# Keys' weights fused in 64x64 tiles at the head of a gated-mix kernel

## Chip, cores and metric

The kernel runs on one core of a Trainium2 chip. The metric is the device time of one execution in microseconds. The engines named below are TensorE (PE in the profile, its weight loads PEld), VectorE (DVE), ScalarE (ACT), GpSimd (POOL) and SyncE (SP), which here only issues DMAs. All are in order, each by its own instruction stream.

## What is computed

x has 2048 rows of 512. Two branches are mixed by a gate that each row computes from itself: a linear attention with 32 heads of 16, and a dense layer with Mish. Everything is fp32.

```python
x = A_x
g = sigmoid((x * gate_w).sum(-1, keepdims=True))
# a: attention
q, k, v = (x @ wqkv) split into 3 parts of 32 heads x 16
pq, pk = q @ w_phi[head], k @ w_phi[head]                  # 16x16 per head
phi_q = concat(softmax(pq), softmax(-pq)); phi_k = likewise of pk
kv = phi_k^T v; z = sum over rows of phi_k
a = ((phi_q kv) / (phi_q z + 1e-6)) @ wo
# b: dense
b = mish(x @ w1 + b1) @ w2
return g * a + (1 - g) * b
```

Only the head of the kernel changes. There the weights of the keys are multiplied by w_phi once ("fuse"), so that x @ (wk w_phi) gives pk directly; the same is done for the queries.

## The kernel before

**Splitting.** A product in fp32 is slower on TensorE than one in the fp32r form. So every operand X is split into a high part Xh (a copy rounded to fp32r, made on ACT) and a low part Xl = X - Xh (a subtraction, on DVE or POOL), and each product is made of three: Xh Wh, Xh Wl and Xl Wh, summed in one PSUM bank.

**Stages.** Stage A goes over 8 chunks of 256 rows of x. Each chunk makes k, v and q (12 products each for two tiles of 128 rows), the softmax features of k, and adds to kv. Stage B goes over 4 blocks of 512 rows: the features of q, the attention's output, and the dense branch. The instruction order within the stages is written out by hand as words (FIRST, EVEN, ... BLOCK); every word runs a step that was registered by `at`. `pin` keeps each instruction in the order of the program on its engine.

**The head**, which is all that the change touches:

- L141 to L165 issue the first loads. `bds` (the block-diagonal w_phi, 256 KB) goes out on ACT's queue. On SP's queue go, in this order, the keys' weights wkT in four parts of 256 KB (one for each 128 of the 512 inputs), with x's first chunk (`rawx[0]`, 512 KB, all four input parts) behind the first two; then wv in two pieces of 512 KB, the queries' weights wqT in four parts, and x's second chunk.
- L168 to L172: `ones` is filled on DVE, and `WARM` = 6 fp32 products of `ones` by `ones` run on TensorE into a PSUM bank that nobody reads. They need nothing but `ones`.
- `fuse(staged, k)` (L213) multiplies part k of the staged weights by bds: four fp32 products of 128x128, one for each group G of 8 heads, into the four quarters of one PSUM bank. `fsplit` (L681) then writes that bank to `wkh[:, k]` (ACT) and the rest to `wkl[:, k]` (DVE).
- `fuse_tiles(staged, ks)` (L219) does two parts of the queries' weights with 64x64 tiles instead: bds is block-diagonal with 16x16 blocks, so only the products of rows r..r+64 with columns r..r+64 of bds are not zero. Each group takes four products of 64x64 (two halves of the contraction, two halves of the output), which lie in four different quarters of the array. The two halves r go to two PSUM banks, and two parts k share the pair.
- `x_hi` and `x_lo` split one half j of x's chunk (two input parts, 128x512) on ACT and on DVE.
- `k_part(k)` (L688) adds input part k to the keys of both row tiles of the first chunk: for each tile Xh Wh, Xh Wl, Xl Wh, six products of 128x512 in all. The two sums stay in PSUM (`pk`) through all four parts.
- The order at L696 to L714: fuse 0, fsplit 0, both halves of x, fuse 1, fsplit 1, fuse 2, fsplit 2, k_part(0), fuse 3, fsplit 3, k_part(1), the splits of wv, k_part(2), k_part(3). `run(FIRST, ...)` follows, with `fq` (the queries' fuse) and v first.

**PSUM.** Eight banks of 128x512 in three pools: tag "a" has 3, "dn" 4, "kv" 1. The warm products and the keys' and queries' fuse use "dn" in turn, `pk` uses "a". A bank is written again only when its readers are done.

Of the kernel before, what the change touches and what calls it, by code (L numbers as in the profile page):

```python
# [15 lines left out]
P = 128  # L16
# [5 lines left out]
NG = 4  # L22
SC = 256
# [7 lines left out]
NF = NFA + NFB  # L31
GROW = FA % P
ORDER = [NFA - 1] + list(range(NFA - 1)) + list(range(NFA, NF))
WARM = 6

# [52 lines left out]
def tile_gated_mix(ctx: ExitStack, tc: tile.TileContext, xT, wv, wkT, wqT, bd, w1a, w1b, b1, w2a, w2b, wo, out):  # L90
# [6 lines left out]
    pin = tc.keep_in_program_order  # L97
    V, G_, A_, Sy = nc.vector, nc.gpsimd, nc.scalar, nc.sync

    def mm(*a, **k):  # L100
        return pin(nc.tensor.matmul(*a, **k))  # L101

    def T(shape, dt, tag, bufs, name):
        nm[0] += 1
        return sp.tile(shape, dt, name=f"{name}_{nm[0]}", tag=tag, bufs=bufs)

    def k8(name, tag, dt=F32R):
        return T([P, 2048], dt, tag, 1, name)

    def k4(name, tag, dt=F32):  # L110
        return T([P, 1024], dt, tag, {"E": 4, "tx": 2, "oh": 2, "z": 1}[tag], name)

    def k2(name, tag, dt=F32):
        return T([P, 512], dt, tag, {"pq": 3, "io": 4, "hl": 8}[tag], name)

    def psum(name, tag, bufs={"a": 3, "dn": 4, "kv": 1}):
        nm[0] += 1
        return pp.tile([P, 512], F32, name=f"{name}_{nm[0]}", tag=tag, bufs=bufs[tag])

    def act(out_, in_, fn=AF.Copy, **k):  # L120
        return pin(A_.activation(out_, in_, fn, **k))  # L121

    def kt(t, f):
        return t[:, : KT * f].rearrange("p (k f) -> p k f", f=f)
# [4 lines left out]
    def f32(ap):  # L129
        return ap.bitcast(F32)  # L130
# [5 lines left out]
    def stage(wT):  # L136
        return T([P, NFA * 512], F32, "w1a", 2, "wT")[:, : KT * 512].rearrange("p (k g f) -> p k g f", k=KT, f=P)

    skT, sqT = stage(wkT), stage(wqT)
    bds = k2("bds", "io")[:, :].rearrange("p (g f) -> p g f", g=NG)  # L140
    pin(A_.dma_start(bds, bd))  # L141
    rawx = {}

    def ldx(c):
        rawx[c] = k4("xraw", "tx")
        pin(Sy.dma_start(kt(rawx[c], SC), xT[c]))

    def ldk(dst, src, k):
        pin(Sy.dma_start(dst[:, k, :, :], src[:, k, :, :]))

    ldk(skT, wkT, 0)
    ldk(skT, wkT, 1)
    ldx(0)
    ldk(skT, wkT, 2)
    ldk(skT, wkT, 3)

    def piece(dram, o, n=1024):
# [9 lines left out]

    ones = k2("ones", "io")[:, :P]  # L168
    pin(V.memset(ones, 1.0))
    ps = psum("warm", "dn")  # L170
    for _ in range(WARM):
        mm(ps[:, :P], ones, ones, start=True, stop=True)  # L172
    onr = const.tile([P, P], F32R, name="onr")
    A_.preload_act_table_set("exp_and_others")
    act(onr, ones)
# [20 lines left out]
    def at(key, name, fn):  # L196
        steps.setdefault((key, name), []).append(fn)

    def run(text, key, prev=None, nxt=None):
# [6 lines left out]
    wkh, wkl, wvh, wvl, wqh, wql = [  # L206
        kt(k8(n, t), 512) for n, t in (("wkh", "xbh"), ("wkl", "xbl"), ("wvh", "woh"), ("wvl", "wol"), ("wqh", "tt"), ("wql", "eT"))]
    xs, Es, vs, psA = {}, {}, {}, {}
# [1 line left out]
    zacc = k4("zacc", "z")  # L210
    pin(G_.memset(zacc, 0.0))

    def fuse(staged, k):  # L213
        acc = psum("fuse", "dn")
        for G in range(NG):
            mm(acc[:, G * P : (G + 1) * P], staged[:, k, G, :], bds[:, G, :], start=True, stop=True)
        return acc

    def fuse_tiles(staged, ks):  # L219

        acc = [psum("fuse", "dn") for _ in range(2)]
        for i, k in enumerate(ks):
            for G in range(NG):
                o = (i * NG + G) * 64
                for r in (0, 64):
                    for c in (0, 64):
                        mm(acc[r // 64][c : c + 64, o : o + 64], staged[r : r + 64, k, G, c : c + 64], bds[r : r + 64, G, r : r + 64], start=True, stop=True, skip_group_check=True)
        return acc

    def proj(x, t, wh, wl, tag):  # L230
        ps = psum("proj", tag)
        xh, xl = x
        sl = slice(t * P, (t + 1) * P)
        n = 0
        for a, w in ((xh, wh), (xh, wl), (xl, wh)):
            for k in range(KT):
                mm(ps, a[k // 2][:, k % 2, sl], w[:, k, :], start=(n == 0), stop=(n == 3 * KT - 1))
                n += 1
        return ps
# [4 lines left out]
    def x_hi(c, j):  # L244
        act(xs[c][0][j], kt(rawx[c], SC)[:, 2 * j : 2 * j + 2, :])

    def x_lo(c, j, eng):
        pin(eng.tensor_sub(xs[c][1][j], kt(rawx[c], SC)[:, 2 * j : 2 * j + 2, :], f32(xs[c][0][j])))
# [189 lines left out]
    def mid_ops():  # L438
# [18 lines left out]
        def z():  # L457
            B["zb"] = k4("zb", "z")
            for a in range(2):
                ps = psum("z", "dn")  # L460
                for j in range(2):
                    mm(ps, onr, B["zs"][j][:, a * 512 : (a + 1) * 512], start=(j == 0), stop=(j == 1))
                act(B["zb"][:, a * 512 : (a + 1) * 512], ps)
# [212 lines left out]
        b_ops(b)  # L676


    acc = {}

    def fsplit(h, l, k):  # L681
        act(h[:, k, :], acc[k])
        pin(V.tensor_sub(l[:, k, :], acc[k], f32(h[:, k, :])))

    new_x(0)
    pk = {}

    def k_part(k):  # L688
        for t in range(2):
            sl = slice(t * P, (t + 1) * P)  # L690
            if t not in pk:
                pk[t] = psum("proj", "a")
            for n, (a, w) in enumerate(((xs[0][0], wkh), (xs[0][0], wkl), (xs[0][1], wkh))):
                mm(pk[t], a[k // 2][:, k % 2, sl], w[:, k, :], start=(k == 0 and n == 0), stop=(k == KT - 1 and n == 2))

    acc[0] = fuse(skT, 0)  # L696
    fsplit(wkh, wkl, 0)
    for j in range(2):
        x_hi(0, j)
        x_lo(0, j, V)  # L700
    acc[1] = fuse(skT, 1)
    fsplit(wkh, wkl, 1)
    acc[2] = fuse(skT, 2)
    fsplit(wkh, wkl, 2)
    k_part(0)
    acc[3] = fuse(skT, 3)
    fsplit(wkh, wkl, 3)
    k_part(1)
    for j in range(2):
        h, l = [w[:, 2 * j : 2 * j + 2, :].rearrange("p k f -> p (k f)") for w in (wvh, wvl)]  # L710
        act(h, wvr[j])
        pin((V, G_)[j].tensor_sub(l, wvr[j], f32(h)))
    k_part(2)
    k_part(3)  # L714

    def fq():
        for j in range(2):
            acc["q", 2 * j], acc["q", 2 * j + 1] = fuse_tiles(sqT, (2 * j, 2 * j + 1))

    at(("A", 0), "fq", fq)  # L720
    for i in range(4):
        j, r = i // 2, i % 2
        wh, wl = [w[:, 2 * j : 2 * j + 2, :].rearrange("p k (g r f) -> p r (k g) f", r=2, f=64)[:, r, :, :] for w in (wqh, wql)]

        def ps(i=i):
            return acc["q", i][:, :].rearrange("p (g f) -> p g f", f=64)

        at(("A", 0), f"fh{i}", lambda wh=wh, ps=ps: act(wh, ps()))
        at(("A", 0), f"fl{i}", lambda wh=wh, wl=wl, ps=ps: pin(V.tensor_sub(wl, ps(), f32(wh))))
# [71 lines left out]
```

## Time and profile before

| | us |
|---|---|
| three runs | 451.97, 452.77, 452.78 |
| their median | 452.77 |
| the profiled execution | 452.07 |
| its span, first to last instruction | 450.3 |
| TensorE's first product (warm) | 1.12 |
| TensorE idle after the warm products | 4.05 to 5.82 |
| queries' fuse, first product | 16.44 |
| first product of v | 18.46 |
| end of TensorE's last product | 447.15 |

The profile's page begins with the busy time of each engine; the trace behind it can be asked for any stretch. A stretch's row gives the busy time and the number of instructions of each engine in it. The chain of waits follows the work that ended last backwards through whatever released each step. A group of instructions shows the tile that is written, the tiles that are read, their shapes, the count, the busy time with the mean duration of one in ns, and the idle time of the engine just before them with what ended it. In this trace an fp32 product appears as two matmul rows (two passes of the array), an fp32r product as one. Rows on TensorE overlap: a row of 0.39 us may be followed by the next one 0.227 us later, so I look at the distance from start to start.

### The profile page before, as it was taken

The page shows a single profiled execution, that of the slowest core. Times are in us where ns is not written, and L with a number is a line of the kernel's source. Part 1 is how long each engine was busy: PE and PEld are TensorE (multiplying, and loading weights), DVE is VectorE, ACT ScalarE, POOL GpSimd, SP SyncE. Part 2 cuts the span into 40 slices and gives each one's busy share as a digit, 9 for nine tenths or more (in the row PEclk, how much of TensorE's full clock was granted, in tenths as well). Part 3 has the DMA queues.
Part 4 walks back from the last instruction along what each step waited for, and adds up shares of the span by engine and source line. Part 5 has one row for each costly group of instructions (what it writes and reads, how often), then busy time and mean ns, then how long its engine had stood idle before and what let it go on. Part 6 is the DMA issues. An engine that isn't in the chain of part 4 may idle for free.

```text
span 450.3 us, 6996 instructions
## 1 busy us (share of the span) xinstructions
PE 444.3 (99%) x2778; PEld 363.6 (81%) x2778; DVE 305.7 (68%) x404; ACT 194.8 (43%) x265; POOL 162.8 (36%) x102
## 2 busy tenths in 40 slices
PE   7999999999999999999999999999999999999997
PEld 6888888888888888878787887887887888787885
DVE  2599459369399999997989976576967629611003
ACT  3544443344335555626265453534254553234221
POOL 3438777767952345521122212024212122221211
DMA  7721514605524100405244151331151302030002
GB/s 281 259 92 48 175 49 130 181 14 182 184 74 119 48 24 20 122 13 140 84 105 130 35 154 34 83 118 48 29 137 46 100 16 95 1 82 13 1 1 93
DMA packets 25737, 40.07 MB, mean 89 GB/s; under 512 B 5732, under 2 KB 14180, under 8 KB 25704
## 3 DMA queue, kind: packets, MB, share of 16 engines
q1 hardware_dynamic: 25384, 39.22, 28.8%
q8 instruction: 22, 0.36, 0.4%
q10 hardware_dynamic: 288, 0.39, 0.3%
q14 instruction: 11, 0.09, 0.1%
q0 software_dynamic: 32, 0.01, 0.0%
HBM read 22.82 MB, written 8.40 MB: 69 GB/s over the span
## 4 chain that ended last, share of the span: by engine, by line
PE 98%; DMA 1%; DVE 0%; issue 0%
PE proj L101 29%; PE up L101 27%; PE down L101 26%; PE wo L101 10%; PE num L101 2%; PE kvp L101 2%; PE fuse L101 2%; DMA bds<-in_bd_dram 1%; PE rest L101 0%; PE z L101 0%; DVE io L651 0%; PE kvT L454 0%
## 5 line engine op out<-in xcount | busy, mean ns | idle before, releaser
L498 POOL TENSOR_TENSOR l<-act,h 128x512 fp32r<-128x512 f32 x44 | 63.0, 1432 | 222.1 <-ACT h L121 183.6
L121 ACT ACTIVATE act<-up,b1s 128x512 f32<-128x512 f32 x44 | 30.3, 688 | 88.9 <-PE up L101 87.7
L318 POOL TENSOR_TENSOR zacc<-zacc,E 128x1024 f32<-128x1024 f32 x16 | 39.7, 2483 | 42.7 <-DVE E L280 32.6
L121 ACT ACTIVATE E<-E 128x1024 f32<-128x1024 f32 x32 | 33.6, 1059 | 47.7 <-DVE E L265 47.6
L280 DVE TENSOR_TENSOR E<-E,Sm 128x1024 f32<-128x1024 f32 x32 | 45.7, 1427 | 1.1
L269 DVE TENSOR_REDUCE Sm<-E 128x64 f32<-128x1024 f32 x32 | 38.7, 1210 | 5.0 <-ACT E L121 5.0
L101 PE MATMUL wo<-woh,ohl 128*128 128x512 f32 x128 | 40.7, 389 | 0.0
L101 PE MATMUL down<-w2ah,h 128*128 128x512 f32 x96 | 37.5, 390 | 0.0
L101 PE MATMUL down<-w2ah,l 128*128 128x512 f32 x96 | 37.4, 389 | 0.0
L101 PE MATMUL down<-w2al,h 128*128 128x512 f32 x96 | 37.3, 389 | 0.0
L256 DVE TENSOR_REDUCE mx<-proj 128x32 f32<-128x512 f32 x16 | 11.0, 689 | 30.7 <-PE proj L101 30.7
L101 PE MATMUL down<-w2bh,h 128*128 128x512 f32 x78 | 30.5, 390 | 0.0
L101 PE MATMUL down<-w2bl,h 128*128 128x512 f32 x78 | 30.4, 389 | 0.0
L101 PE MATMUL down<-w2bh,l 128*128 128x512 f32 x78 | 30.3, 389 | 0.0
L121 ACT ACT_TABLE_LOAD x19 | 24.4, 1283 | 10.1 <-PE up L101 9.8
L121 ACT ACTIVATE h<-act 128x512 fp32r<-128x512 f32 x44 | 27.8, 632 | 1.4
L610 DVE TENSOR_TENSOR ohl<-num,ohl 128x512 fp32r<-128x512 f32 x16 | 10.3, 682 | 26.5 <-ACT ohl L121 26.3
L101 PEld LDWEIGHTS wo<-woh,ohl 128*128 128x128 f32 x128 | 24.0, 188 | 5.0
L101 PE MATMUL up<-xbh,w1ah 128*128 128x512 f32 x96 | 26.2, 394 | 0.0
L101 PE MATMUL up<-xbh,w1al 128*128 128x512 f32 x96 | 25.7, 389 | 0.0
L101 PE MATMUL up<-xbl,w1ah 128*128 128x512 f32 x96 | 25.7, 389 | 0.0
L403 DVE TENSOR_TENSOR xbl<-xraw,xbh 128x1024 fp32r<-128x1024 f32 x8 | 12.2, 1563 | 19.8 <-ACT xbh L121 19.8
(121 smaller groups left out, 969.7 us busy)
## 6 DMA issues: line engine op xcount, KB each, us to landing
xraw<-in_xT_dram SPq DMA_DIRECT2D x16, 512.0 KB, 4.7
eT<-tt SPq DMA_DIRECT2D x128, 64.0 KB, 2.0
pqd<-qs SPq DMA_DIRECT2D x16, 256.0 KB, 3.0
pq<-pqd SPq DMA_DIRECT2D x16, 256.0 KB, 2.9
out_dram<-io SPq DMA_DIRECT2D x15, 256.0 KB, 2.1
raw<-in_w1a_dram SPq DMA_DIRECT2D x3, 512.0 KB, 4.5
raw<-in_w2a_dram SPq DMA_DIRECT2D x3, 512.0 KB, 3.8
wT<-in_wkT_dram SPq DMA_DIRECT2D x4, 256.0 KB, 5.5
```

Of the source, the lines that this page charges most:

```text
L101: return pin(nc.tensor.matmul(*a, **k))
L121: return pin(A_.activation(out_, in_, fn, **k))
L256: pin(V.tensor_reduce(d[name], hv(src()), axis=AX.X, op=op))
L269: pin(V.tensor_reduce(d["S"], hv(d["E"][:, :]), axis=AX.X, op=ALU.add))
L280: pin(eng.tensor_mul(hv(d["E"][:, :]), hv(d["E"][:, :]), d["S"][:, :, None].to_broadcast([P, 2 * H, DH])))
L318: at(key, f"z{t}", lambda d=d: pin(G_.tensor_add(zacc, zacc, d["E"])))
L403: pin(V.tensor_sub(xb[b][1][:, :, sl], kt(raw[h], SC), f32(xb[b][0][:, :, sl])))
L498: pin(G_.tensor_sub(U[i]["l"], U[i]["a"], f32(U[i]["h"])))
L610: pin(V.tensor_sub(ohl[h, gp][:, 512:], num[h, gp], f32(ohl[h, gp][:, :512])))
```

## The change

The keys' fuse is made of 64x64 tiles, as the queries' fuse is. `fuse` now does one part k of either into a pair of banks that the caller passes (`fuse_banks`), at the half of the columns that k's parity gives. The keys take a pair of their own for each part, though a part fills only the left or the right half of the two; the queries still put two parts into one pair. `fsplit` empties a part in two ACT copies and two DVE subtractions of 128x256, one for each bank, instead of one of each of 128x512.

x's first chunk is loaded in two halves, between the first three parts of wkT. Ten warm products run ahead of the fuse instead of six, and two more between the keys' parts 0 and 1. The bank of the warm products comes from pool "a".

The head's order is new: fuse 0, two warm products, fuse 1; half 0 of x, fsplit 0, half 1 of x, fsplit 1; k_part(0), k_part(1); fuse 2, fuse 3, fsplit 2, fsplit 3; the splits of wv, k_part(2), k_part(3). Within k_part the order is Xh Wh for both tiles, Xl Wh for both, Xh Wl for both. In the built program each engine's order behind the head is the old one. One DMA more is issued on SP, and since the DMAs share eight semaphores in turn, wv's second piece now waits on SP for the landing of bds, and each later load for the landing of another earlier one than before.

```diff
-WARM = 6
+WARM = 10
...
     ldk(skT, wkT, 0)
-    ldk(skT, wkT, 1)
-    ldx(0)
-    ldk(skT, wkT, 2)
+    rawx[0] = k4("xraw", "tx")
+    for j in range(2):
+        pin(Sy.dma_start(kt(rawx[0], SC)[:, 2 * j : 2 * j + 2, :], xT[0][:, 2 * j : 2 * j + 2, :]))
+        ldk(skT, wkT, j + 1)
     ldk(skT, wkT, 3)
...
-    ps = psum("warm", "dn")
-    for _ in range(WARM):
-        mm(ps[:, :P], ones, ones, start=True, stop=True)
+    pw = psum("warm", "a")
+
+    def warm(n):
+        for _ in range(n):
+            mm(pw[:, :P], ones, ones, start=True, stop=True)
+
+    warm(WARM)
...
-    def fuse(staged, k):
-        acc = psum("fuse", "dn")
+    def fuse(acc, staged, k):
+
         for G in range(NG):
-            mm(acc[:, G * P : (G + 1) * P], staged[:, k, G, :], bds[:, G, :], start=True, stop=True)
-        return acc
...
+            o = (k % 2 * NG + G) * 64
+            for r in (0, 64):
+                for c in (0, 64):
+                    mm(acc[r // 64][c : c + 64, o : o + 64], staged[r : r + 64, k, G, c : c + 64], bds[r : r + 64, G, r : r + 64], start=True, stop=True, skip_group_check=True)
+
+    def fuse_banks():
+        return [psum("fuse", "dn") for _ in range(2)]
+
+    def halves(w, ks):
+        return [w[:, ks, :].rearrange("p k (g r f) -> p r (k g) f", r=2, f=64)[:, r, :, :] for r in range(2)]
...
-    def fsplit(h, l, k):
-        act(h[:, k, :], acc[k])
-        pin(V.tensor_sub(l[:, k, :], acc[k], f32(h[:, k, :])))
+    def fsplit(acc, k):
+        wh, wl = halves(wkh, slice(k, k + 1)), halves(wkl, slice(k, k + 1))
+        src = [a[:, k % 2 * 256 : k % 2 * 256 + 256].rearrange("p (g f) -> p g f", f=64) for a in acc]
+        for r in range(2):
+            act(wh[r], src[r])
+        for r in range(2):
+            pin(V.tensor_sub(wl[r], src[r], f32(wh[r])))
...
     def k_part(k):
-        for t in range(2):
-            sl = slice(t * P, (t + 1) * P)
-            if t not in pk:
-                pk[t] = psum("proj", "a")
-            for n, (a, w) in enumerate(((xs[0][0], wkh), (xs[0][0], wkl), (xs[0][1], wkh))):
+        for n, (a, w) in enumerate(((xs[0][0], wkh), (xs[0][1], wkh), (xs[0][0], wkl))):
+            for t in range(2):
+                sl = slice(t * P, (t + 1) * P)
+                if t not in pk:
+                    pk[t] = psum("proj", "a")
                 mm(pk[t], a[k // 2][:, k % 2, sl], w[:, k, :], start=(k == 0 and n == 0), stop=(k == KT - 1 and n == 2))
 
-    acc[0] = fuse(skT, 0)
-    fsplit(wkh, wkl, 0)
-    for j in range(2):
-        x_hi(0, j)
-        x_lo(0, j, V)
-    acc[1] = fuse(skT, 1)
-    fsplit(wkh, wkl, 1)
-    acc[2] = fuse(skT, 2)
-    fsplit(wkh, wkl, 2)
-    k_part(0)
-    acc[3] = fuse(skT, 3)
-    fsplit(wkh, wkl, 3)
-    k_part(1)
+    for ks in ((0, 1), (2, 3)):
+        acc = []
+        for k in ks:
+            acc.append(fuse_banks())
+            fuse(acc[-1], skT, k)
+            if k == 0:
+                warm(2)
+        for k in ks:
+            if k < 2:
+                x_hi(0, k)
+                x_lo(0, k, V)
+            fsplit(acc[k % 2], k)
+        if ks[0] == 0:
+            k_part(0)
+            k_part(1)
...
     def fq():
         for j in range(2):
-            acc["q", 2 * j], acc["q", 2 * j + 1] = fuse_tiles(sqT, (2 * j, 2 * j + 1))
+            accq.extend(fuse_banks())
+            for k in (2 * j, 2 * j + 1):
+                fuse(accq[-2:], sqT, k)
```

## The prediction

> **What bounds the kernel now.** I read the page's first part, then stretches of the span chosen at the seams of the kernel's head, then the chain of waits over the first 20 us. Columns of the stretches: length, each engine's busy us and (instructions), granted clock, DMA share, GB/s.
>
> ```profile
> PE 444.3 (99%) x2778; PEld 363.6 (81%) x2778; DVE 305.7 (68%) x404; ACT 194.8 (43%) x265; POOL 162.8 (36%) x102
> ...
> 0.00:5.80 5.80, 2.93 (x12) 2.63 (x12) 0.17 (x1) 1.59 (x2) 3.58 (x13) 1.00 0.57 164
> 5.80:8.50 2.70, 2.68 (x12) 2.68 (x13) 0.00 (x0) 0.57 (x2) 0.00 (x0) 1.00 1.03 403
> 8.50:16.40 7.90, 7.90 (x46) 6.68 (x44) 5.01 (x7) 4.64 (x8) 1.38 (x1) 1.00 1.01 377
> 16.40:18.40 2.00, 2.00 (x129) 1.96 (x128) 0.14 (x1) 0.77 (x2) 1.09 (x1) 1.00 0.76 231
> 18.40:447.20 428.80, 428.75 (x2593) 349.62 (x2582) 299.90 (x396) 187.21 (x254) 156.71 (x88) 1.00 0.27 79
> 447.20:450.40 3.20, 0.00 (x0) 0.00 (x0) 0.47 (x1) 0.00 (x0) 0.00 (x0) 1.00 0.46 164
> ```
>
> TensorE is the bound without a gap: from 18.40 to 447.20 it is busy 428.75 of 428.80 us, and already from 5.82. The change touches only what comes before 18.4 us. So the question is how much sooner TensorE reaches the queries' fuse and, behind it, the first v product. Columns of the chain: start, us, what.
>
> ```profile
> 0.81 4.97 DMA bds<-in_bd_dram
> 5.78 0.04 issue
> 5.82 4.30 PE fuse L101 x24
> 10.13 1.40 PE proj L101 x6
> 11.52 0.89 PE fuse L101 x8
> 12.41 4.09 PE proj L101 x18
> 16.51 2.02 PE fuse L101 x128
> ```
>
> The fp32 fuse product is two passes of the array, so a part k of the keys' fuse is 4 products, 8 passes; a proj product is one pass. The last part took 0.89 us, 0.112 a pass. The first three took 4.30 for 24: in the single rows passes start 0.213 us apart until 8.54, then 0.112. The warm products, 12 passes in 2.93 us, also start 0.213 apart. So TensorE ran at 1/1.9 of its speed until 8.54, though the granted clock stands at 1.00 in every stretch; I go by the spacing. Proj products start 0.227 apart. The queries' fuse is already made of 64x64 tiles: 128 passes, four parts, in 2.02.
>
> Counted in slots (when TensorE can begin the next product), the keys' path runs from 5.82 to 16.35, the last proj's start at 16.12 plus 0.227.
>
> **The change, part by part.** The sum goes along TensorE's order, from 5.82.
>
> *Twelve warm products.* Ten stand ahead: 20 passes, first step 0.37, then 0.213, free at 5.55. That lies under the wait for bds, which lands at 5.78: cost nothing. Were they 0.3 us longer, that would be paid in full. A quicker clock only ends them sooner. Two more, 4 passes x 0.112 = 0.45, follow part 0.
>
> *64x64 tiles.* In the queries' fuse four passes start together every 0.0585, eight such steps a part: 0.47 instead of 0.89. Going in from proj costs 0.14 (slot 16.35; 32 steps later it ends at 18.36, 2.01 less 1.87), and coming out costs 0.24 (from 18.36 the eighth v product starts at 20.185 instead of 19.95). Both are paid three times more: around part 0, around part 1, around parts 2 and 3. Bounds of a pair: 0, if the next operand is waited for anyway, to 0.76, twice the row. I take 0.38.
>
> *x in halves.* SP now issues wkT 0, x half 0, wkT 1, x half 1, wkT 2, wkT 3.
>
> ```profile
> xraw<-in_xT_dram SPq DMA_DIRECT2D x3, 512.0 KB, 6.5
> wT<-in_wkT_dram SPq DMA_DIRECT2D x4, 256.0 KB, 5.5
> ...
> 0.80 0.87 SPq L149 DMA_DIRECT2D wT<-in_wkT_dram  x2
> 1.72 0.43 SPq L146 DMA_DIRECT2D xraw<-in_xT_dram  x1
> ```
>
> wkT 1 landed at 6.76, x at 1.72 + 6.5 = 8.21; the 512 KB of x took 1.45. Halved: x half 0 at 6.76, wkT 1 at 7.48, x half 1 at 8.21; wkT 2 and 3 as before. Behind it SP has one issue more (0.45): wv 0 goes out that much later, wv 1 now waits for bds's semaphore, 5.8 instead of 4.08, and the four wqT and x's second chunk follow it. That is free: by 5.80 only 5.80 x 164 GB/s = 0.95 MB of the 2.25 MB issued had moved, and the queues stay full for 3.2 us at 403 GB/s. Without that cover the last wqT (landed at 14.84, wanted at 16.9) has 2 us to lose.
>
> *Evictions in halves.* Each part leaves in two ACT copies and two DVE subtractions of 128x256 instead of one of each of 128x512: four more on each engine.
>
> ```profile
> L121 ACT ACTIVATE wkh<-fuse 128x512 fp32r<-128x512 f32 x4 | 2.4, 594 | 6.9 <-PE fuse L101 6.8
> L121 ACT ACTIVATE wvh<-raw 128x1024 fp32r<-128x1024 f32 x2 | 2.0, 1052 | 0.0
> L121 ACT ACTIVATE onr<-ones 128x128 fp32r<-128x128 f32 x1 | 0.3, 311 | 0.0
> ...
> L683 DVE TENSOR_TENSOR wkl<-fuse,wkh 128x512 fp32r<-128x512 f32 x4 | 2.7, 687 | 8.9 <-ACT wkh L121 8.9
> ```
>
> No 128x256 copy is in the trace. ACT: between 0.311 (128 columns) and 0.594 (512); on the line to 1.052, 0.38, and 0.29 from one start to the next (512 columns start 0.50 apart). DVE: between 0.165 (ones, 128 columns) and 0.687; on the line to wvl's 1.226, 0.42, and 0.33 apart instead of 0.60. The Trainium skill ("TensorEngine Tiling (Array Packing)", Performance Considerations) warns that tiles speed up TensorE but not what empties PSUM, and advises wide accesses over tiles of one bank. With it the extra evictions become the bound; that is the first rival, priced from the rows alone. The trace does not show it so far: behind the queries' fuse TensorE goes on with v and waits for no copy.
>
> *The walk.* Part 0: 5.82 + 0.14 + 0.47 = 6.43. Out, two warm products: 7.12. Wait for wkT 1 (7.48 + 0.04): 7.52. Part 1, in and out: 8.37. k_part(0) needs the copy of x half 0 (6.80 to 7.42), wkh 0 (two copies, 7.97) and wkl 0 (8.8, wanted at 9.3): all there. Six products x 0.227: 9.73. k_part(1) needs wkh 1; on ACT its two copies stand behind the copy of x half 1, which waits for 8.21, so they end at 9.4. wkl 1, on DVE behind x half 1's subtraction, ends at 10.24, wanted at 10.64. 11.09. Parts 2 and 3: 0.14 + 0.94 = 12.17, out at 12.41; their PSUM banks were freed by wkl 0 and wkl 1. wkh 2 starts once part 2 is out of the array (11.70 + 0.16 + 0.04) and ends 0.67 later at 12.57: TensorE waits till 12.62. Twelve products: 15.34. That is 1.0 sooner than 16.35.
>
> *Behind it.* From there the order is the old one on every engine. DVE is free at 15.25 and waits 3.0 us for wqh. The low part of wv's second half is done on POOL at 17.49 and is wanted 6 products after the v product's start (18.46 + 1.4), 1.4 later. x's second chunk (issued at 8.91, 6.5 to land) is there long before ACT takes it at 19.56. So the 1.0 us reaches the end: the profiled execution is 452.07, 1.7 more than its span, and 452.07 - 1.0 = **451.1**. The runs' median, 452.77, lies 0.7 above this execution. If TensorE merely reached its speed 1.5 us later there (each us costs 1 - 1/1.9 = 0.47), that is the 0.7, and the changed kernel would not have it. No trace shows it.
>
> **The clock of the warm-up.** The rows: 2.93 us of unbroken products from 1.12 did not raise the speed; 2.72 us from 5.82 did. After the change the work is unbroken from 1.12 to 5.55 and goes on at 5.82, so I expect the rise before 7.1, where it costs nothing, since waits of 0.40 and 0.21 us follow. Each later us costs 0.47 beyond 0.6 us of such waits: a rise at 8.54, as now, gives 1.0 - (2.72 x 0.47 - 0.6) = 0.3 gained, 451.7. By the Trainium skill ("TensorE: Matmul & The Clock Gate", Part 1: The HAM clock gate) about 3.4 us of sustained work in a free-running window raise it, and the moment differs from run to run. Such a window fits by 1.12 + 6.8 = 7.9 at the latest: an estimate of 451.5 at worst (2.1 x 0.47 - 0.6 = 0.4 lost). This trace differs in that 2.72 us sufficed.
>
> **The rivals.**
> 1. *Evictions become the bound.* If a half costs what a whole one does (0.594 and 0.50 apart on ACT, 0.687 and 0.60 on DVE), wkh 1 is ready at 9.9, wkl 1 at 11.2 instead of 10.24. Parts 2 and 3 then start at 11.7, wkh 2 is ready at 13.6, DVE's wkl 3 at 15.6, and the queries' fuse starts at 16.4 to 16.5: nothing gained, **452.1**. For: ACT and DVE are strictly in order here and have 12 and 11 pieces between 6.8 and 14. Against: the rows grow with the columns.
> 2. *TensorE stays slow, the other side.* The first part, two warm products and part 1 are broken by a wait and three changes of tile size, so the speed may not rise in this stretch. It decides from a rise at 5.82 + 1.6 / 0.47 = 9.2. At 14: 8.9 us of work lie on the path, 8.2 us at 1/1.9 do 4.3 of it, the rest ends at 18.6: 2.3 later, **454.3**. For: 12 slow passes did not suffice once. Against: there are now 20.
> 3. *The waits vanish.* If leaving and entering tiles costs nothing beside the waits, three pairs and the last wait go: 1.0 + 0.4 to 0.9, so **450.5**. For: bds and wkT 1 are waited for anyway. Against: the change at 18.46 shows 0.24 with nothing waited for.
> 4. *It does not do what it says:* x half 0 lands no sooner than the whole x did (8.21). Then part 0's copies stand behind it on ACT until 9.4 and k_part(0) starts at 9.5 instead of 8.37: the 1.0 is gone, **452.1**. For: the queues are at 403 GB/s, shared with bds. Against: wkT 1, in the same place, landed at 6.76.
>
> **How the numbers follow.** The forecast 0.60 (alone 450.6 to 451.8); rival 1 0.13, rival 2 0.10, rival 3 0.10, rival 4 0.07. This kernel's runs tell some 0.2%, 0.9 us, from no change: faster is below 451.86. Forecast and rival 3 lie there, with a quarter of rival 1's and 4's spread: 0.75. Rival 2 is slower beyond 453.68 in two thirds of its cases: 0.07. The rest, 0.18, is the same. The range leaves out most of rival 2 and the far end of rival 3, and takes in rivals 1 and 4 with half of the 0.7 by which other runs lay higher: 450.4 to 452.6.
>
> **What would show it.** In the profile after: a warm stretch without a gap to 5.6; passes 0.112 apart before part 1; x half 0 landed near 6.8 and wkT 1 near 7.5; the first proj near 8.4, the last of the keys' products near 15.1; the queries' fuse near 15.4; TensorE gapless from there. A first proj after 9, DVE busy without a gap from 7.4 to 14, or passes 0.213 apart after 8 would prove the forecast wrong, each for its own rival.

## The result and the profile after

Six runs of each kernel: 452.77 us before (451.97 to 453.57), 451.06 after (450.54 to 451.64). The ratio is 0.9965, its 95% interval 0.9953 to 0.9977: 1.7 us faster. The profiled execution after took 451.0, with a span of 449.3.

The same stretches of the profile after, with the seams where they now lie (stretch, length, busy us and instructions of PE, PEld, DVE, ACT and POOL, granted clock, DMA share, GB/s):

```profile
0.00:5.80 5.80, 4.21 (x20) 4.01 (x20) 0.17 (x1) 1.59 (x2) 3.58 (x13) 1.00 0.55 174
5.80:8.50 2.70, 2.48 (x71) 2.14 (x72) 1.32 (x3) 1.64 (x4) 0.00 (x0) 1.00 1.04 402
8.50:15.40 6.90, 6.62 (x92) 4.95 (x93) 4.04 (x9) 3.81 (x9) 0.59 (x1) 1.00 1.02 367
15.40:17.40 2.00, 2.00 (x129) 1.93 (x129) 0.28 (x1) 0.91 (x2) 1.88 (x1) 1.00 0.97 307
17.40:446.00 428.60, 428.60 (x2582) 349.72 (x2582) 299.74 (x395) 187.08 (x254) 156.97 (x88) 1.00 0.27 80
```

TensorE has no gap behind the head here either. From the first v product to the last product it takes 428.69 us, as it did before (18.46 to 447.15, now 17.32 to 446.00). In all fourteen profiles of this study that distance lies between 428.68 and 428.71. So the start of the first v product tells what the head of a profiled execution is worth, free of all that comes behind it.

The chain of waits after (start, us, what):

```profile
0.80 5.17 DMA bds<-in_bd_dram
...
6.02 0.69 PE fuse L101 x32
6.71 0.64 PE warm L101 x4
7.36 0.63 PE fuse L101 x32
7.98 3.00 PE proj L101 x12
10.98 0.64 PE fuse L101 x32
11.61 0.02 issue
11.64 0.67 ACT wkh L121 x2
12.30 0.04 issue
12.35 3.02 PE proj L101 x12
15.36 2.02 PE fuse L101 x128
```

At full speed the eight passes of an old part took 0.89; a part with the change of tile size now takes 0.63 to 0.69. Parts 2 and 3 follow the products of parts 0 and 1, and behind them stands the one wait on this stretch: TensorE needs the copies of part 2 in wkh, which are not ready. It costs 0.28 us, as the single row says:

```profile
12.35 0.73 PE L101 MATMUL proj<-wkh,xh 128*128 128x512 f32 x2 [0.28 <-ACT wkh L121]
```

The copies to wkh and the subtractions to wkl, in the groups of the first 16 us (count, busy us, mean ns, idle time of the engine just before them):

```profile
L687 DVE TENSOR_TENSOR wkl<-fuse,wkh 128x256 fp32r<-128x256 f32 x8 | 2.9, 416 | 2.0 <-ACT wkh L121 2.0
...
L121 ACT ACTIVATE wkh<-fuse 128x256 fp32r<-128x256 f32 x8 | 2.5, 380 | 2.4 <-PE fuse L101 2.4
```

### The profile page after: what moved, and what is told of

It is laid out like the page before. It is cut to its first block, busy times and chain, and to the rows that moved or that the text cites. A ratio compares the mean times of both kernels' runs of the same rounds, so it can differ in the third digit from the quotient of the medians.

```text
span 449.3 us, 7222 instructions
## 1 busy us (share of the span) xinstructions
PE 443.9 (99%) x2886; PEld 362.8 (81%) x2886; DVE 306.0 (68%) x408; ACT 195.0 (43%) x269; POOL 163.0 (36%) x102
## 4 chain that ended last, share of the span: by engine, by line
PE 98%; DMA 1%; ACT 0%; DVE 0%; issue 0%
PE proj L101 29%; PE up L101 27%; PE down L101 26%; PE wo L101 10%; PE num L101 2%; PE kvp L101 2%; DMA bds<-in_bd_dram 1%; PE fuse L101 1%; PE rest L101 0%; PE z L101 0%; ACT wkh L121 0%; PE warm L101 0%; DVE io L653 0%; PE kvT L456 0%
```

## The experiments

All twelve runs, behind the first two kernels, with the start of the first proj and of the first v product in the profiled execution, and the median and range of the timed runs. Each ratio is to the runs of the kernel before on the same chip. Their median was 452.51 on the chip of the rows from "six warm products ahead" to "x whole", 452.88 from "changed, again" to "wait covered, small bds", and 452.64 on that of the last four rows.

| kernel | first proj | first v | median us (range), runs | ratio, 95% |
|---|---|---|---|---|
| before, first profile | 9.88 | 18.46 | 452.77 (451.97 to 453.57), 6 | |
| changed, first profile | 7.91 | 17.32 | 451.06 (450.54 to 451.64), 6 | 0.9965, 0.9953 to 0.9977 |
| six warm products ahead | 8.06 | 18.74 | 452.94 (451.09 to 455.09), 12 | 1.0009, 0.9993 to 1.0025 |
| before, ten warm products | 9.35 | 17.95 | 451.58 (451.40 to 451.82), 12 | 0.9983, 0.9974 to 0.9991 |
| whole products | 8.53 | 18.11 | 451.41 (451.03 to 451.79), 9 | 0.9973, 0.9963 to 0.9983 |
| x whole | 9.27 | 18.69 | 452.32 (451.76 to 452.55), 11 | 0.9993, 0.9984 to 1.0003 |
| changed, again | 7.68 | 17.07 | 450.94 (450.81 to 451.41), 7 | 0.9959, 0.9944 to 0.9974 |
| no middle products | 7.60 | 17.86 | 451.82 (451.28 to 452.71), 12 | 0.9979, 0.9967 to 0.9991 |
| wait covered | 8.41 | 17.47 | 450.75 (450.32 to 451.15), 6 | 0.9954, 0.9938 to 0.9971 |
| wait covered, small bds | 8.09 | 17.10 | 450.64 (450.41 to 452.53), 10 | 0.9957, 0.9943 to 0.9970 |
| no middle, twelve ahead | 7.64 | 17.03 | 450.98 (450.62 to 451.32), 11 | 0.9964, 0.9951 to 0.9976 |
| no middle, second look | 7.73 | 17.99 | 452.24, 1 | |
| before, second look | 9.77 | 18.36 | 451.95, 1 | |
| before, third look | 10.66 | 19.26 | 452.88, 1 | |

### Six warm products ahead

```diff
-WARM = 10
+WARM = 6
```

> The changed kernel with six warm products ahead instead of ten (the two in the middle stay). Theory: the longer warm-up is what brings TensorE to full speed before the keys' fuse; with six, passes stay 0.213 us apart until about 8.5, parts 0 and 1 and the two middle products take 0.4 us more each, the first proj starts near 9.0 instead of 7.91, and the median is 0.7 to 1.1 us above the changed kernel's 451.06 (451.8 to 452.2). Rival: the warm-up only fills idle time; the speed rises by 7 all the same and the time stays at 451.1 within 0.2.

Measured: 452.94, above the 451.8 to 452.2 of the theory, with runs from 451.09 to 455.09. The best is level with the changed kernel's median, the worst is slower than any run of before. The profiled execution shows one way (stretch, length, TensorE's busy us and rows, granted clock, DMA share, GB/s):

```profile
0.00:4.10 4.10, 2.93 (x12) 1.00 0.41 85
4.10:5.90 1.80, 0.00 (x0) 1.00 1.01 368
5.90:7.40 1.50, 1.48 (x48) 1.00 1.03 378
7.40:10.90 3.50, 3.50 (x39) 0.51 1.04 413
10.90:16.00 5.10, 4.82 (x81) 1.00 0.99 376
```

Here the speed was up when the keys' fuse began (its tiles start 0.058 apart from the second step on) and fell to a clock of one half for 3.4 us, in which proj products stood 0.427 apart. It had been 1.8 us idle just before the fuse. So my theory was right in that six are too few, and wrong in how: in this execution the speed did not rise late, it fell back. Without the longer warm-up the rest of the change shows no gain in the median (ratio 0.9993 to 1.0025).

### The kernel before with ten warm products

```diff
-WARM = 6
+WARM = 10
```

> The kernel before with ten warm products ahead and nothing else. Theory: the speed rises near 4.6, the three first fuse parts pass in 0.9 us each or wait for their loads, but x still lands at 8.2 and part 2's weights near 8.9, so the first proj starts between 9.7 and 9.9 as it did (9.88), and the profiled span stays within 0.3 us of 450.3. If the 0.7 us by which the runs of before lie over their profiled execution comes from later rises of the speed, the median falls from 452.77 to about 452.0 and the spread of the runs to below 0.8. Rival A: the warm-up alone brings 1 us or more (median 451.7 or less). Rival B: the 0.7 has another cause: median stays at 452.8.

The median fell from 452.51 on that chip to 451.58, and the range from 2.1 us (33 runs) to 0.4. The theory was right on the spread and wrong on the rest: it had a median of about 452.0, the first proj at 9.7 to 9.9 (it came at 9.35) and the span within 0.3 of 450.3 (it was 449.8). Rival A was nearer: the median is below its 451.7, though the gain is 0.9 and not 1. The chain of waits, from 2.19 on:

```profile
2.19 6.20 DMA wT<-in_wkT_dram
8.39 0.04 issue
8.44 1.16 PE fuse L101 x8
9.59 1.38 PE proj L101 x6
10.98 0.89 PE fuse L101 x8
11.87 4.13 PE proj L101 x18
15.99 2.02 PE fuse L101 x128
```

With TensorE at speed its head is bound by a load: part 2 of the weights, which it fuses before any product, lands at 8.39. In the second look at the kernel before, below, it landed at 8.8, and the first v product came 0.4 us later than here.

### Whole products

```diff
...
-        for r in range(2):
-            act(wh[r], src[r])
-        for r in range(2):
-            pin(V.tensor_sub(wl[r], src[r], f32(wh[r])))
+        act(wkh[:, k, :], acc)
+        pin(V.tensor_sub(wkl[:, k, :], acc, f32(wkh[:, k, :])))
...
-            acc.append(fuse_banks())
-            fuse(acc[-1], skT, k)
+            acc.append(fuse_whole(skT, k))
```

`fuse_whole` is the old `fuse`, one bank a part.

> The changed kernel with the keys' fuse in whole 128x128 products again (one bank a part, one copy and one subtraction of 128x512), the rest of the change as it is. Theory: a part costs 0.89 us instead of 0.47 + 0.38 for the change of tile size, so the first proj starts near 8.25 instead of 7.91, parts 2 and 3 take 1.8 instead of 1.1 but hide the wait for wkh 2; TensorE reaches the queries' fuse near 15.5 instead of 15.2, 0.3 us later (median 451.2 to 451.5). Rival: the tiles carry the gain: four times 0.42 us, median 452.5 or more.

451.41, in the range of the theory and far from the rival's 452.5. The tiles are worth some 0.4 us, not four times 0.42: much of what they save goes into entering and leaving them three times, and some into the wait for wkh 2. The profiled execution was its slowest run, with slow passes until 6.75.

### x whole

```diff
-    rawx[0] = k4("xraw", "tx")
-    for j in range(2):
-        pin(Sy.dma_start(kt(rawx[0], SC)[:, 2 * j : 2 * j + 2, :], xT[0][:, 2 * j : 2 * j + 2, :]))
-        ldk(skT, wkT, j + 1)
+    ldk(skT, wkT, 1)
+    ldx(0)
+    ldk(skT, wkT, 2)
```

> The changed kernel with x's first chunk loaded whole behind the second part of wkT, as before. Theory: x lands at 8.2; on ACT the keys' copies stand behind the copy of x's first half, so wkh 0 is ready near 9.4 and the first proj starts near 9.5 instead of 7.91; the queries' fuse starts near 16.6, 1.3 to 1.6 us later, and all of the gain is gone (median 452.3 to 452.7). Rival: x's halves are hidden by the work before them; within 0.3 us of 451.06.

452.32: as the theory said, the gain is gone; the 0.2 us that are left are not clear of nothing (ratio 0.9984 to 1.0003). The chain of waits:

```profile
1.72 6.30 DMA xraw<-in_xT_dram
8.02 0.02 issue
8.04 0.63 ACT xh L121
8.67 0.56 ACT wkh L121 x2
9.23 0.04 issue
9.27 3.03 PE proj L101 x12
```

The first proj waits for ACT, and ACT for x: in ACT's order the copies of part 0, which TensorE had finished by 6.7, stand behind the copy of x.

This is also 0.7 us slower than the old head with ten warm products (451.58 on the same chip). There the copies of part 0 go ahead of x. So part of the 1.3 us between this and the changed kernel is likely what the new order costs when x lands whole; the new order alone, and the halves of x in the old order, were not run.

### No middle products, and the changed kernel beside it

```diff
-            if k == 0:
-                warm(2)
```

> The changed kernel itself, beside the next three on one chip. Theory (the clock decides the spread): its first warm product to the first proj stays without a long pause, so the speed never falls back; runs within 450.5 to 451.7, median 451.1, while runs of before spread over 2 us. Rival: the first six runs were lucky; some runs above 452.5 as in the kernel with six warm products.

> The changed kernel without the two warm products between the keys' parts 0 and 1. By the sum they cost nothing, since part 1's weights land near 7.2 and TensorE would only wait. Theory A: they are filling against the clock: TensorE idles 0.7 us before part 0 and 0.5 more before part 1, and in some runs the speed falls back as with six warm products; the median rises by 0.2 to 0.6 and the slowest runs pass 452.5. Theory B: they have no effect; the first proj starts 0 to 0.1 us sooner (7.8 to 7.9) and the median stays within 0.15 of the changed kernel's. Theory C: they delay part 1; the median falls by 0.2 or more.

The changed kernel gave 450.94 again, with no run above 451.41. Without the two middle products it is 451.82. By the size that is theory A or more, but not by its cause. The passes of part 0 are slow in this execution (the steps of its tiles are 0.107 apart, and 0.058 from part 1 on), but part 1 waits until 6.91 for its weights all the same, and the first proj comes at 7.60, 0.08 sooner. The time is lost eight microseconds later. The chain of waits, from the queries' fuse:

```profile
15.06 0.90 PE fuse L101 x49
15.96 0.58 issue
16.54 1.39 PE fuse L101 x79
```

TensorE stands for 0.58 us in the middle of the queries' fuse. From its first product to the first v product the queries' fuse takes 2.87 us, where the changed kernel's takes 2.03. All weights had landed by 14.9, and the row names no releaser. What differs is the queue that brings instructions. In the page of before its row is

```profile
q8 instruction: 22, 0.36, 0.4%
```

That is 22 packets of 16 KB, 65 bytes for each of TensorE's 2 x 2778 rows, so I take it for TensorE's own program. In the DMA rows of 9.0 to 13.9 (queue, packets, MB, share) the changed kernel's second run has a packet

```profile
q8 instruction: 1, 0.02, 1.4%
```

and the kernel without the middle products has none there; it has one in 13.9 to 16.0:

```profile
q8 instruction: 1, 0.02, 3.0%
```

The packets themselves start at 10.75 and at 14.21.

### Twelve ahead, none in the middle; a second look

```diff
-WARM = 10
+WARM = 12
```

This is an edit of the kernel without middle products.

> No warm products in the middle, but twelve ahead: as many instructions on TensorE ahead of the queries' fuse as in the changed kernel, with the pause before part 1 left open. Theory (instructions): the 0.58 us for which TensorE stood in the queries' fuse of the kernel without middle products, with no tile or semaphore to wait for, is late instructions: a 16 KB block of its program was fetched only at 14.2 there, at 10.8 and 12.0 in the changed kernel. With the count restored the stall is gone and the median is 451.0 to 451.3 (the longer warm-up may end up to 0.4 us behind bds in some runs). Rival (filling): the pause before part 1 is what costs, by the clock; median 451.6 or more, slow passes or a clock below 1.0 behind 7 us.

> A second look at the kernel without the middle products. Theory (instructions): the block is again fetched after 13 us and TensorE stands 0.3 us or more in the queries' fuse with no releaser. Rival: the stall was a chance of one execution; fetched near 11 to 12, no stall, first v product near 17.0.

Both went as the theory of instructions said. With the count restored, the packet started at 10.78, nothing stalled, and the median is 450.98, the changed kernel's. In the second look at the kernel without them it started at 14.15, and the stall is there again:

```profile
15.22 0.90 PE fuse L101 x49
16.12 0.55 issue
16.67 1.39 PE fuse L101 x79
```

Both times TensorE stops behind the same product, the 49th pass of this fuse. The kernels without middle products start this fuse at 15.0 with the stall (first look) and without it (twelve ahead), so the clock of the head is not the cause. The two middle products are worth nothing where they stand, but they shift the program by eight instructions (four matmul rows and four weight loads), and with the count restored elsewhere the early fetch is back.

That the stop is a wait for this packet is inferred: the packet's own row ends at 15.2, and TensorE goes on only at 16.5. Why eight instructions fewer move the start of the fetch to 14.2 (two profiles) is open; with the full count it lies between 10.75 and 12.03 (five). It is no plain count either: the kernel with six warm products has eight instructions fewer still, its packet started at 13.79, and it did not stall, since it came to the queries' fuse only at 16.72.

The stall is not all of the 0.88 us between 451.82 and 450.94. By the spans of the runs it is 0.55 (449.75 against 449.2); the rest lies outside the span. There all runs of the changed kernel and of the kernel before spend 1.7 to 1.8 us, seven of the twelve without the middle products 2.0 to 3.0. In the second look, with 2.2 us outside, the last packet of that queue starts at 451.6, 1.7 us behind the last instruction; in both profiles of the changed kernel it starts before 442. The profile with six warm products shows the same (452.5, and 2.4 us outside). That the one causes the other is not shown.

### The kernel before, two more looks

> A second look at the kernel before. Theory (clock): its runs spread over 2 us because the moment differs at which the speed rises, or because it falls back after the pause of 1.8 us behind the warm products; the first v product moves with it (18.46 at a time of 452.07), by as much as the time does within 0.2. Rival: head as in the first profile and a different time, so the spread comes from elsewhere.

> A third look at the kernel before, with the same expectations: the first v product's start and the time move together (theory), or do not (rival).

Time and first v product move together. Third look: 452.88, 0.81 more than the first profile; first v product 0.80 later. Its chain of waits:

```profile
0.81 4.98 DMA bds<-in_bd_dram
...
5.83 5.08 PE fuse L101 x24
10.90 1.38 PE proj L101 x6
```

The first 24 passes took 5.08 instead of 4.30: they stood 0.213 apart until 10.26, not 8.54. The second look is the other end. All passes but the first step of each run of fuse products are 0.112 apart, from 5.95 on, and yet it gained only 0.1 us, since TensorE then waits 0.9 us for wkT 2.

### Two versions that might be better

The first moves the last pair of k_part(1) into the wait for wkh 2:

```diff
-    def k_part(k):
-        for n, (a, w) in enumerate(((xs[0][0], wkh), (xs[0][1], wkh), (xs[0][0], wkl))):
+    def k_part(k, ns=(0, 1, 2)):
+        for n in ns:
+            a, w = ((xs[0][0], wkh), (xs[0][1], wkh), (xs[0][0], wkl))[n]
...
+            if k == 3:
+                k_part(1, (2,))
...
-            k_part(1)
+            k_part(1, (0, 1))
```

> The changed kernel with the last two products of k_part(1) moved behind the keys' parts 2 and 3, so that they lie in the wait for wkh 2 (0.28 us in the profile). Theory: the wait is gone, the queries' fuse starts 0.25 to 0.35 sooner (near 15.0 instead of 15.29) and the median falls to 450.7 to 450.9. Rival: the wait moves on to wkl 2 or wkl 3 on DVE, which stand in the same row, and nothing is gained.

The second has this too, and loads of bds only the half that the tiles read, with nine warm products instead of ten (the products then take `bds[r : r + 64, G, :]`):

```diff
-WARM = 10
+WARM = 9
...
-    bds = k2("bds", "io")[:, :].rearrange("p (g f) -> p g f", g=NG)
+    bds = k2("bds", "io")[:, : NG * 64].rearrange("p (g f) -> p g f", g=NG)
...
+    bd = np.ascontiguousarray(np.concatenate([bd[:64, :, :64], bd[64:, :, 64:]]))
```

> The kernel of the last run with bds loaded without the blocks that the tiles never read (128 KB instead of 256 KB) and nine warm products ahead instead of ten, so that they end before it. Theory: TensorE waits for bds and wkT 0 together, which share the queues; 128 KB less at 0.4 MB/us bring part 0 and every later load 0.3 us sooner, part 0 near 5.6 instead of 6.0, and the queries' fuse near 14.7; median 450.4 to 450.6, faster than both kernels. Rival: wkT 0, issued at the same time, lands no sooner (5.8), or the copies on ACT bind; gain over the last run below 0.1.

In the first the wait is gone from the chain: 14 products follow the tiles without a gap. The queries' fuse still starts at 15.44, and not near 15.0.

```profile
8.48 2.53 PE proj L101 x10
11.02 1.09 PE fuse L101 x64
12.11 3.40 PE proj L101 x14
15.51 2.02 PE fuse L101 x128
```

In the second, part 0 starts at 5.63, 0.1 to 0.4 sooner than in the other profiles of the changed head with ten ahead; but with the whole of bds it started at 5.51 in the kernel before with ten warm products, so this too may be scatter. The medians are 450.75 and 450.64, beside 450.94 for the changed kernel on that chip; but the intervals overlap almost wholly, the second had one run at 452.53, and both were profiled in executions whose passes were slow until about 7, so that their first v products (17.47 and 17.10) came no sooner than the changed kernel's 17.07. Both beat the kernel before. That they beat the changed one is not shown.

## Why the prediction was right, and where it was lucky

**The bound and the carry-through.** Right: what the head gains at the first v product (18.46 to 17.32, 1.14) TensorE keeps to its last product (447.15 to 446.00), to 0.01 us. The tail behind that was 0.1 longer, so the profiled executions differ by 1.07, where the sum had 1.0.

**The walk.** Step by step, forecast and measured: part 0's first product at 5.82 and 6.02 (bds landed 0.2 later); the end of the middle products at 7.12 and 7.19; part 1's first product at 7.52 and 7.29; the end of k_part(1) at 11.09 and 10.82; the wait for wkh 2 0.21 and 0.28; the last keys' product ends its slot at 15.34 and 15.20. The largest error is wkT 1: I had it at 7.48 and so 0.40 us of waiting, it landed at 7.16 and nothing waited. From part 0's first product the path took 9.18 us, where the sum had 9.52, and that wait accounts for the difference. The late bds hid more than half of it, so that 451.0 came so close to 451.1 is in part luck. In the second profile of the changed kernel bds landed at 5.74, near the forecast's 5.78, and the first v product came 1.4 us sooner than in the first profile of before, not 1.0.

**Evictions.** Right: 380 and 416 ns for a half, where I had 0.38 and 0.42 (the line through the rows of 512 and 1024 columns gives 0.37 for the first). Rival 1 falls: DVE is idle 2.0 us before its subtractions of parts 2 and 3. The Trainium skill's warning ("TensorEngine Tiling (Array Packing)", Performance Considerations) that emptying PSUM may become the bound holds in one place, the 0.28 us for wkh 2.

**x in halves.** Right, and the part on which the gain hangs most after the warm-up: without it 1.3 us are lost (452.32), where rival 4 had 1.0. x half 0 was on ACT at 6.52 where I had 6.80.

**Tiles.** The pair of 0.38 for entering and leaving was about right. In the single rows after, entering parts 2 and 3 costs 0.14 (two starts 0.317 apart instead of 0.227, then 0.107 instead of 0.058), and leaving part 1 0.20 (0.148 instead of 0.058, then 0.339 instead of 0.227), with nothing waited for: rival 3 falls. By the sum the tiles gain 0.04 for each of parts 0 and 1 (0.89 less 0.47 and 0.38) and 0.46 for parts 2 and 3, less the wait of 0.21: 0.33. Whole products cost 0.35 to 0.47 us in the median (451.06 and 450.94 against 451.41).

**The clock.** Right that the speed rises sooner, and understated. I priced the ten products at nothing because they lie under the wait for bds. They do, but what they prevent is worth the most: with six the kernel is not faster than before (ratio 1.0009), and ten of them alone bring 0.9 us in the kernel before. The prices of the parts of the change, 1.9 for the warm-up, 1.3 for x and 0.4 for the tiles in the changed kernel, do not add up to its 1.7: each was taken away with the others in place. I put the 0.7 between the profiled execution of before and its median down to a later rise, and said that no trace showed it; the third look shows it, 0.80 at the first v product for a rise some 1.7 us later, and 1.7 x 0.47 is 0.8. So the medians differ by 1.7 and the profiled executions by 1.1: that of before was one of its quicker runs. Rival 2 is no part of the changed kernel, whose 13 runs end at 451.64, but something like it is what the profile with six warm products shows. I had the rise before 7.1; over the profiles of the changed head with ten or more ahead it came between 4.6 and 7.3.

**What I missed.** That an added product can change when a block of instructions is fetched. It cost nothing here, since the two middle products happen to set the fetch right. That was luck: the sum only counted their time, and without them the kernel is 0.9 us slower.

## What to carry to other kernels

Where one engine is busy to the end, its arrival at the steady part is the whole of the head's worth: read the start of the first steady instruction beside the time, and look for what differs outside the span when the two disagree. Keep TensorE working through the long first wait of a head: in the kernel before four fp32 products more brought 0.9 us and narrowed the spread of the runs from 2.1 us to 0.4. If a stall has no tile and no semaphore behind it, look at the queue that brings the instructions before you blame the data, and try another count of instructions ahead of it.

## What the hardware showed beyond that

- In the profile with six warm products a pause of 1.8 us stood behind 2.9 us of work. TensorE's clock was 1.00 when work went on, fell to 0.50 1.6 us later, and stayed there for 3.4 us. The second look at the kernel before had the same pause and no slow pass behind it, so the pause alone does not decide. The Trainium skill ("TensorE: Matmul & The Clock Gate", Part 1: The HAM clock gate) speaks of free-running windows of about 3.4 us after which the speed is set anew; the length of the slow stretch and the spread from run to run agree with it. It asks for a whole busy window to rise and an idle one to fall; here 2.7 us of work behind the pause (the kernel before, first profile) sufficed for the one, and 1.8 us of idleness for the other.
- The granted clock read 1.00 in stretches in which passes stood 0.213 instead of 0.112 us apart, at the start of all of the profiles. The spacing is the surer sign.
- A block of TensorE's program, 16 KB, which its rows in the page put at some 250 instructions (0.36 MB for 2 x 2778), was fetched while the data queues were full. Started at 14.2, it was followed in two profiles by a stall until 16.5 and 16.7; started between 10.75 and 12.89, in six profiles of the changed head with tiles, by none.
